# The last group of a fused convolution and MLP kernel: evictions shared by two engines, two closings halved

## The chip, the cores and the metric

The kernel runs on one core of a Trainium2 chip. The metric is the device time of one execution in microseconds. Five engines matter: TensorE (PE; its weight loads are shown as PEld), VectorE (DVE), ScalarE (ACT), GpSimd (POOL, which here computes a little and issues the accumulating transfers), and SyncE (SP, which issues plain transfers). TensorE writes its results to PSUM, eight banks of 512 float32 words in each partition; VectorE and ScalarE carry them from there to SBUF.

## What is computed

A causal convolution over 7 positions with one softmaxed set of taps per head, then a layer norm, an MLP with relu, and a residual sum, all in float32, for 8 sequences of 4224 positions and 192 channels:

```python
def _attn_ref(x, weight):
    ...
    w = np.exp(weight - np.max(weight, axis=-1, keepdims=True))
    w = w / (np.sum(w, axis=-1, keepdims=True) + 1e-09)
    ...
    out = np.einsum('hk,bskhg->bshg', w, x_unf)

def _moe_ref(x, g_ln, w_ch1, w_ch2):
    mu = np.mean(x, axis=-1, keepdims=True)
    var = np.mean((x - mu) ** 2, axis=-1, keepdims=True)
    xn = (x - mu) / np.sqrt(var + 1e-06) * g_ln
    ch = np.maximum(xn @ w_ch1, 0.0) @ w_ch2
    return (x + ch).astype(np.float32)
```

`w_ch1` is 192 x 768 and `w_ch2` is 768 x 192.

## The kernel before

The positions are cut into groups, most of them 16 rows for each of 128 partitions. The groups run one after another through two stages on TensorE: *up* (the product with `w_ch1`, then relu) and *down* (the product with `w_ch2`). While TensorE works on group g, VectorE runs the convolution of group g + 1, ScalarE starts that of g + 2, and POOL and SP move data. The order of every instruction is written out by hand: each engine takes its own in the order of the program, and waits that follow from the data are put in where one engine needs another's result.

From the fourth group on, both stages use a scheme of seven block products instead of eight (of the Strassen kind). In `up_mixed` the hidden matrix is split into four quarters c11, c12, c21, c22, all in one large buffer, `room`. Every product goes into a set of four PSUM banks, X or Y in turn (`take_set`, all eight banks in two sets). The seven products are made twice: in pass *one* for a small part of the hidden width (`n` = 1 block of 128, 1024 words a partition over four banks), in pass *two* for the rest (`n` = `PAIR` = 2 blocks, 2048 words a partition).

Three helpers of `Pass` take a product out of its banks. `evict` (L640) copies it to `room` on ScalarE, with a relu or without. `close` (L644) adds it to a quarter that is there already: with `part` = None VectorE adds straight from PSUM (L648); with a `part` ScalarE copies to that room, and POOL issues a transfer that adds the room to the quarter (`add_by_dma`, L609). `relu` (L655) is ScalarE's, in place. `seen` gives the view of the banks, whole or one block f of it; block f lies in columns 256 f to 256 f + 255 of each of the four banks.

The two rooms of pass two (L693) use the buffers of the tiles "cs" and "tb". "cs" also holds the down results of the previous group until `finish_fast` (called from `ahead`, L986) has added the last parts (L897) and transposed them (L899) into `ots`. This runs between the passes: `next(ahead)` stands at L691.

In the last group (`last`) there is no next group, so VectorE has no convolution to run. c11 (L698) and c22 (L722) of pass two are closed by VectorE whole, each 2048 words from PSUM. In the middle of pass two VectorE also multiplies the previous group's result by the norm's factors (L709), and POOL adds it to the output in HBM in four transfers of 384 KB (`add_to_out`, L925); the transfers that POOL issues, these and `add_by_dma`, share one queue.

After that `down_fast` runs seven products too, over quarters of the hidden matrix. Each goes through `product` (L830), in three chunks c, each with a bank. The first uses c11 and the second `a[:, 1, 0]`, which is relu(c21) less c11 (`lower_sum`, L811). The third, on `a[:, 1, 1]` = relu(c22), accumulates over the banks of the second, so it has to wait until ScalarE has copied the second's result (L841). Then VectorE makes nine sums of quarters (`half_sum`, L802) for the last products. Four rows are kept out of the scheme (`keep`, L749) and computed plainly at the very end (L772), where `add` (L929) and `store` (L936) finish.

Of the kernel before, what the change touches and what calls it, by code (L numbers as in the profile page):

```python
# [10 lines left out]
AF = mybir.ActivationFunctionType  # L11
ALU = mybir.AluOpType
# [4 lines left out]
def kernel(  # L17
# [29 lines left out]
    nc = tc.nc  # L47
# [35 lines left out]
    PAIR = NF // 2 - 1  # L83
# [10 lines left out]
    def rows_of_out(g, j1, j2):  # L94

        b, j0, n = groups[g]
        if b is not None:
            return [(slice(0, P), outr[b, :, (j0 + j1) * D : (j0 + j2) * D])]
        left = out[:, P * R : S].rearrange("b (p r) d -> b p (r d)", p=LP)
        return [  # L100
            (slice(LP * b, LP * b + LP), left[b, :, j1 * D : j2 * D]) for b in range(B)
        ]
# [22 lines left out]
    def take_set():  # L125
        i = (turn[0] + 3) // 4 * 4 % 8
        turn[0] = i + 4
        return all_banks[:, i : i + 4]
# [357 lines left out]
    def store_y(g, queue=nc.sync):  # L486
        n = groups[g][2]
        for ps, rows in rows_of_out(g, 0, n):
            queue.dma_start(out=rows, in_=y[g][ps, 0:n].rearrange("p j d -> p (j d)"))
# [118 lines left out]
    def add_by_dma(dst, src):  # L608
        nc.gpsimd.dma_start(out=dst, in_=src, accum_op=ALU.add)  # L609

    def up_mixed(g, ahead, pending):
# [3 lines left out]
        last = g + 1 == NG  # L615
# [7 lines left out]
        class Pass:  # L623
# [15 lines left out]

            def evict(self, banks, dst, relu=False, f=None):  # L640
                src = self.seen(banks, f)
                nc.scalar.activation(dst, src, AF.Relu) if relu else nc.scalar.copy(dst, src)  # L642

            def close(self, c, banks, part=None, f=None):  # L644


                if part is None:
                    nc.vector.tensor_tensor(c, c, self.seen(banks), op=ALU.add)  # L648
                    return
                self.evict(banks, part, f=f)  # L650
                whole = "p f q w -> p (f q w)"
                add_by_dma(c.rearrange(whole), part.rearrange(whole))
# [4 lines left out]
        def parts(pool, tag):  # L657

            room = pool.tile([P, J * D], F32, tag=tag, name=f"parts_{tag}{g}")
            return room.rearrange("p (f q w) -> p f q w", q=NQ, w=W)  # L660

        def act_scales(j1, j2):
            if not last:
                scale(g - 1, j1, j2)

        def taps_of_next(*args, **kw):
            if not last:
                conv(g + 1, *args, **kw)


        X, Y = take_set(), take_set()
        one, two = Pass(PAIR, FC, X, Y), Pass(0, PAIR, Y, X)
        p = one
# [18 lines left out]
        p = two  # L692
        rooms = parts(cpool, "cs"), parts(bpool, "tb")  # L693
        p.product(Y, a11, p.b11, True, False)
        p.evict(Y, p.c11)
        p.product(X, a12, p.b21)
        if last:
            p.close(p.c11, X)  # L698
        else:
            for f in range(PAIR):  # L700
                p.close(p.c11[:, f : f + 1], X, rooms[0][:, f : f + 1], f)
            if g == 3:
                store_y(g, nc.gpsimd)
        act_scales(0, 1)
        if last:

            for j1 in (0, HJ):
                part, factor = ots[g - 1][:, j1 : j1 + HJ], rstd[g - 1][:, j1 : j1 + HJ]
# [10 lines left out]
        p.product(Y, s1, p.b12, False, False)  # L719
        taps_of_next(2, 5)  # L720
        taps_of_next(5, 6, heads=(0, H // 2))
        p.close(p.c22, Y, None if last else rooms[1][:, 0:PAIR])  # L722
        p.product(X, a22, p.t[2], False)
        for f in range(PAIR):
            p.relu(p.c11[:, f : f + 1])
# [8 lines left out]
        p.product(Y, s4, p.b22, False)  # L734
        p.evict(Y, p.c12, True)
        if last:
            p.relu(p.c22)
        lower_sum(g, range(PAIR))
        if last:

# [65 lines left out]
    def lower_sum(g, fs=range(FC)):  # L806

        a = of_products(g)
        if g in MIXED:
            for f in fs:  # L810
                nc.vector.scalar_tensor_tensor(  # L811
                    out=a[:, 1, 0, f], in0=a[:, 1, 0, f], scalar=0.0, in1=a[:, 0, 0, f],
                    op0=ALU.max, op1=ALU.subtract,
                )
        else:
            half_sum(g, (1, 0), (1, 0), (0, 0), ALU.subtract, fs)
# [174 lines left out]
    for g in range(NG):  # L991
        mixed, last = g in MIXED, g + 1 == NG
        if g + 2 < NG and g not in (1, 2, 3):
            load_x(g + 2)
        if mixed:
            work = up_mixed(g, ahead(g), pending)
            pending = iter(())
        else:
            up(g)
            work = []  # L1000
# [90 lines left out]
```

## Time and profile before

| What | Value |
|---|---|
| Median of 3 runs | 957.46 us (956.49 to 957.8) |
| The profiled execution, in all | 959.62 us |
| Its span, first to last instruction | 957.5 us |
| TensorE matmuls busy | 950.6 us (99%) |
| VectorE busy | 890.7 us (93%) |
| ScalarE busy | 696.6 us (73%) |
| POOL busy | 338.4 us (35%) |
| Up stage of the last group, on TensorE | 896.62 to 924.91 us |
| Down stage of the last group, on TensorE | 924.91 to 953.67 us |
| VectorE in pass two of the last group | first closing at 911.76 us, idle 8.01 us before it |

Times inside the profile are counted from the start of the span. "PE busy" says little, since matmuls are pipelined; the wait ahead of a weight load and the time from one product to the next say more. "L648" is line 648 of the kernel. In a timeline row "[0.29 <-DVE room L648]" means that the engine was idle for 0.29 us and that VectorE's write of `room` on that line ended the wait.

### The profile page before, as it was taken

To read this page: it belongs to the slowest core of one execution; us is meant where nothing else is said; L and a number is where in the kernel's file an instruction comes from. 1 tells how busy PE (TensorE), PEld (TensorE's weight loads), DVE (VectorE), ACT (ScalarE), POOL (GpSimd) and SP (SyncE) were. 2 spreads that over 40 slices of the span, in tenths; PEclk is the share of its full clock that TensorE was granted. 3 is DMA by queue.
4 is the path that set the end of the run, shared out by engine and by line. 5 is a ranking of instruction groups with operands and counts; after the bars stand their busy time and mean duration, and the time that the engine had idled before them with its cause. 6 is when DMAs were issued, how large, how long until landed. Compare 5 with 4: busy or idle time off the path is not lost.

```text
span 957.5 us, 37878 instructions
## 1 busy us (share of the span) xinstructions
PE 950.6 (99%) x16858; PEld 743.1 (78%) x16858; DVE 890.7 (93%) x1489; ACT 696.6 (73%) x1165; POOL 338.4 (35%) x472
## 2 busy tenths in 40 slices
PE   9999999999999999999999999999999999999998
PEld 8998896876869697787968778695867769586787
DVE  7999999999999998999999999999999999999757
ACT  6853678596877959687795968779695877967462
POOL 1058422623145141533227141452316232261310
PEclk9999999999999999999999999999999999999999
DMA  8359589689697988979697896969889696778251
GB/s 204 101 160 212 98 230 280 121 187 229 135 263 138 249 156 181 224 132 277 127 249 151 196 220 127 278 131 252 155 197 205 124 276 132 175 136 138 42 96 68
DMA packets 39544, 168.82 MB, mean 176 GB/s; under 512 B 4437, under 2 KB 8150, under 8 KB 33367
## 3 DMA queue, kind: packets, MB, share of 16 engines
q0 software_dynamic: 32576, 106.25, 59.8%
q1 hardware_dynamic: 6800, 60.16, 17.3%
q8 instruction: 132, 2.16, 0.9%
q14 instruction: 30, 0.25, 0.1%
q10 hardware_dynamic: 6, 0.00, 0.0%
HBM read 38.93 MB, written 50.33 MB: 93 GB/s over the span
## 4 chain that ended last, share of the span: by engine, by line
PE 97%; POOL 1%; DMA 1%; ACT 0%; issue 0%; DVE 0%; ACTq 0%; POOLq 0%
PE ps L533 47%; PE ps L835 44%; PE ps L772 4%; PE ps L367 1%; DMA room<-room 1%; PE ps L326 1%; ACT room L642 0%; POOL room L609 0%; POOL d L460 0%; PE ps L354 0%; POOL r L483 0%; POOL d L479 0%; DVE yt L428 0%; POOL d L478 0%; PE ps L335 0%
## 5 line engine op out<-in xcount | busy, mean ns | idle before, releaser
L417 DVE SCALAR_TENSOR_TENSOR y<-xg,taps,y 128x384 f32<-128x384 f32 (+3 forms) x720 | 364.8, 583 | 1.9 <-DMA y<-room 1.3
L835 PE MATMUL ps<-room,w2sums 128*32 128x256 f32 (+2 forms) x4608 | 247.4, 371 | 0.0
L533 PE MATMUL ps<-yt,w 32*128 32x256 f32 (+2 forms) x4104 | 234.8, 378 | 0.3 <-DVE yt L428 0.3
L642 ACT COPY room<-ps 128x1024 f32<-128x1024 f32 (+1 forms) x135 | 175.0, 1296 | 78.6 <-PE ps L533 77.8
L533 PEld LDWEIGHTS ps<-yt,w 32*128 32x128 f32 x4104 | 204.1, 185 | 25.8 <-issue 8.7
L835 PEld LDWEIGHTS ps<-room,w2sums 128*32 128x32 f32 x4608 | 153.5, 110 | 87.8 <-ACT room L655 5.3
L835 PE MATMUL ps<-room,w 128*32 128x256 f32 (+2 forms) x3456 | 189.8, 371 | 0.1
L802 DVE TENSOR_TENSOR room<-room 128x1024 f32<-128x1024 f32 (+2 forms) x147 | 161.2, 1172 | 22.7 <-PE ps L835 16.1
L835 PEld LDWEIGHTS ps<-room,w 128*32 128x32 f32 x3456 | 113.9, 110 | 67.9 <-DVE room L648 5.0
L533 PE MATMUL ps<-ysums,w1sums 32*128 32x256 f32 x2160 | 125.3, 379 | 0.2 <-issue 0.2
L533 PEld LDWEIGHTS ps<-ysums,w1sums 32*128 32x128 f32 x2160 | 109.1, 185 | 11.2 <-ACT room L642 3.6
L925 POOL DMA_DIRECT2D out_dram<-ot x69 | 58.9, 940 | 159.3 <-ACT ot L914 102.6
L409 POOL DMA_DIRECT2D y<-tb x59 | 52.4, 1384 | 155.0 <-ACT room L841 110.2
L841 ACT COPY cs<-ps 128x256 f32<-128x256 f32 (+2 forms) x192 | 70.2, 367 | 45.6 <-PE ps L835 45.5
L655 ACT ACTIVATE room<-room 128x1024 f32<-128x1024 f32 (+1 forms) x89 | 92.5, 1072 | 0.8 <-DMA room<-parts_cs 0.8
L914 ACT ACTIVATE ot<-ot,r 128x192 f32<-128x192 f32 x224 | 90.9, 464 | 0.0
L380 ACT ACTIVATE y<-xg,taps 128x384 f32<-128x384 f32 (+3 forms) x141 | 73.1, 608 | 0.2 <-DMA xg<-in_x_dram 0.2
L448 DVE BATCH_NORM_STATS2 st<-y 128x6 f32<-128x192 f32 x264 | 70.1, 344 | 0.0
L841 ACT COPY room<-ps 128x256 f32<-128x256 f32 (+2 forms) x96 | 35.5, 369 | 46.5 <-PE ps L835 43.8
L398 ACT ACTIVATE tb<-xg,taps 128x384 f32<-128x384 f32 (+1 forms) x120 | 66.0, 627 | 0.0
L533 PE MATMUL ps<-yt,w1sums 32*128 32x256 f32 x1080 | 65.3, 380 | 0.4 <-ACT room L642 0.4
L533 PE MATMUL ps<-ysums,w 32*128 32x256 f32 x1080 | 64.6, 376 | 0.0
(113 smaller groups left out, 918.0 us busy)
## 6 DMA issues: line engine op xcount, KB each, us to landing
xg<-in_x_dram SPq DMA_DIRECT2D x14, 2112.0 KB, 16.6
room<-room POOLq DMA_DIRECT2D x45, 512.0 KB, 5.1
out_dram<-ot POOLq DMA_DIRECT2D x59, 384.0 KB, 9.6
y<-tb POOLq DMA_DIRECT2D x58, 384.0 KB, 8.5
out_dram<-y SPq DMA_DIRECT2D x13, 1536.0 KB, 9.5
room<-parts_cs POOLq DMA_DIRECT2D x28, 512.0 KB, 6.8
room<-parts_tb POOLq DMA_DIRECT2D x14, 1024.0 KB, 7.6
xg<-in_x_dram POOLq DMA_DIRECT2D x1, 2112.0 KB, 13.6
```

The lines of the kernel that those rows point to most:

```text
L380: nc.scalar.mul(y[g][:, 0:n, cs], xg[g][:, 0:n, cs], taps[:, h, 0:1])
L398: nc.scalar.mul(tb[g][:, 0:n, cs], xg[g][:, 1 : 1 + n, cs], taps[:, h, 1:2])
L417: nc.vector.scalar_tensor_tensor(out=y[g][:, 0:n, cs], in0=t[:, k : k + n, cs], scalar=taps[:, h, k : k + 1], in1=y[g][:, 0:n, cs], op0=AL ...
L448: nc.vector.bn_stats(out=sums[g][:, j, :], in_=y[g][:, j, :])
L533: nc.tensor.matmul(banks[:, q, i * w : i * w + w], right[rows, c, P * i : P * i + P], left[rows, :, c, :], start=(first and c == 0 and i = ...
L642: nc.scalar.activation(dst, src, AF.Relu) if relu else nc.scalar.copy(dst, src)
L655: nc.scalar.activation(c, c, AF.Relu)
L802: nc.vector.tensor_tensor(a[:, *dst, f], a[:, *left, f], a[:, *right, f], op=op)
L835: nc.tensor.matmul(dst[C * q : C * q + C, 0:w], right[:, f, C * c : C * c + C], left[:, f, q], start=(first and f == PAIR), stop=(f == PAI ...
L841: nc.scalar.copy(to[:, c], dst[:, 0:w].rearrange("p (j t) -> p j t", t=t))
L914: nc.scalar.mul(ots[g][:, j, :], ots[g][:, j, :], rstd[g][:, j : j + 1])
L925: nc.gpsimd.dma_start(out=rows[:, d0:d1], in_=src[:, d0:d1], accum_op=ALU.add)
```

## The change

All of it concerns the last group. In pass one each eviction is cut in two by banks: ScalarE takes banks 0 and 1 of the set, VectorE banks 2 and 3, with relu or without; a closing of pass one, which evicts into a room first, is cut the same way. In pass two the closings of c11 and c22 are cut by blocks f: VectorE adds block 0 from PSUM, and ScalarE copies block 1 to a room, from which a transfer on POOL's queue adds it. The relu of c22 is made per block. Because VectorE takes its instructions in order, L897 and L899 of the previous group now come behind its evictions of pass one.

```diff
             def evict(self, banks, dst, relu=False, f=None):
                 src = self.seen(banks, f)
+                if last and self.n == 1:
+                    near, far = [[v[:, :, q : q + 2] for v in (dst, src)] for q in (0, 2)]
+                    if relu:
+                        nc.scalar.activation(*near, AF.Relu)
+                        nc.vector.tensor_scalar_max(*far, 0.0)
+                    else:
+                        nc.scalar.copy(*near)
+                        nc.vector.tensor_copy(*far)
+                    return
                 nc.scalar.activation(dst, src, AF.Relu) if relu else nc.scalar.copy(dst, src)
...
                 if part is None:
-                    nc.vector.tensor_tensor(c, c, self.seen(banks), op=ALU.add)
+                    nc.vector.tensor_tensor(c, c, self.seen(banks, f), op=ALU.add)
                     return
...
         p.product(X, a12, p.b21)
-        if last:
-            p.close(p.c11, X)
-        else:
-            for f in range(PAIR):
-                p.close(p.c11[:, f : f + 1], X, rooms[0][:, f : f + 1], f)
-            if g == 3:
-                store_y(g, nc.gpsimd)
+        for f in range(PAIR):
+            part = None if last and f == 0 else rooms[0][:, f : f + 1]
+            p.close(p.c11[:, f : f + 1], X, part, f)
+        if g == 3:
+            store_y(g, nc.gpsimd)
...
-        p.close(p.c22, Y, None if last else rooms[1][:, 0:PAIR])
+        if last:
+            for f in range(PAIR):
+                p.close(p.c22[:, f : f + 1], Y, rooms[1][:, f : f + 1] if f else None, f)
+        else:
+            p.close(p.c22, Y, rooms[1][:, 0:PAIR])
...
         p.evict(Y, p.c12, True)
         if last:
-            p.relu(p.c22)
+            for f in range(PAIR):
+                p.relu(p.c22[:, f : f + 1])
         lower_sum(g, range(PAIR))
```

## The prediction, made before the changed kernel was run

> **What bounds the kernel now.** I read the busy shares first, then the chain of work that ended last, then the timeline of the last group (896 us to the end), then the landing times of its transfers.
>
> ```profile
> PE 97%; POOL 1%; DMA 1%; ACT 0%; issue 0%; DVE 0%; ACTq 0%; POOLq 0%
> ```
>
> TensorE carries 97% of the chain that sets the end. The last pieces of that chain, in order of time (start, us, engine, tile, line, matmul records):
>
> ```profile
> 859.89 9.28 PE ps L533 x172
> 869.17 27.44 PE ps L835 x504
> 896.62 28.29 PE ps L533 x504
> 924.91 20.76 PE ps L835 x504
> 945.66 8.01 PE ps L772 x48
> ```
>
> Undisturbed up records take 9.28/172 = 54.0 ns each, so 504 cost 27.2 us. The last group's 504 take 28.29: about 1.1 us of waiting lies in the whole up stage, and that is nearly all there is to win. The timeline (start, us, engine, line, operation, tiles, form, idle before and its releaser) shows the places:
>
> ```profile
> 898.03 0.94 DVE L897 TENSOR_TENSOR cs<-cs,room 128x768 f32<-128x768 f32 x1
> 898.19 1.01 ACT L642 COPY room<-ps 128x1024 f32<-128x1024 f32 x1 [1.14 <-PE ps L533]
> 899.01 1.90 DVE L899 STREAM_TRANSPOSE ot<-cs 128x512 f32<-128x512 f32 x3
> 899.25 1.18 PEld L533 LDWEIGHTS ps<-ysums,w1sums 32*128 32x128 f32 x24 [0.24 <-ACT room L642]
> ...
> 911.45 5.53 PE L533 MATMUL ps<-ysums,w1sums 32*128 32x256 f32 x96
> 911.76 2.29 DVE L648 TENSOR_TENSOR room<-room,ps 128x2048 f32<-128x2048 f32 x1 [8.01 <-PE ps L533]
> 913.97 3.42 DVE L709 TENSOR_TENSOR ot<-ot,r 128x1536 f32<-128x1536 f32 x2
> 914.10 2.47 PEld L533 LDWEIGHTS ps<-ysums,w1sums 32*128 32x128 f32 x48 [0.29 <-DVE room L648]
> ...
> 926.75 1.90 ACT L655 ACTIVATE room<-room 128x2048 f32<-128x2048 f32 x1
> ...
> 927.90 6.06 PE L835 MATMUL ps<-room,w2sums 128*32 128x192 f32 x144
> 928.55 0.97 ACT L841 COPY cs<-ps 128x192 f32<-128x192 f32 x4
> ...
> 933.74 7.91 DVE L802 TENSOR_TENSOR room<-room 128x768 f32<-128x768 f32 x9 [6.62 <-ACT kept L749]
> ```
>
> The reader should see four things. A set of four banks is handed back to TensorE some 0.05 us after its eviction ends (898.19 + 1.01 = 899.20, weights at 899.25). VectorE runs the previous group's sums and transposes (L897, L899) during pass one. ScalarE applies the relu to c22 at 926.75 and copies the first down results only behind it. And from 927.90 to the end TensorE has no gap worth naming, while VectorE starts its nine half sums when the third down product has ended and is busy without a break into the last stores. So whatever shifts that third product shifts the end by as much.
>
> **Pass one.** Its seven products are 24 records each, 7 x 24 x 54 ns = 9.07 us. It runs from 896.55 to 906.27 (911.45 less 96 records of the next pass), 9.72 us. So 0.65 us can go if the bank sets come back sooner. Seven ScalarE evictions of 1024 at 1.01 become 14 of 512. ScalarE: 1.01 for 1024 and 1.87 for 2048 give 0.86 per 1024 plus 0.15, so 0.58. VectorE: reading a bank it takes 2.29 for 2048 and 0.35 for 192 (L875), 1.045 ns an element, so 0.68; its bounds are 0.35, the shorter of these reads, and 1.01, the whole eviction of today. With 0.68 each set is back 0.33 us earlier, more than the 0.1 us each product waits. I take the full -0.65; at 1.01 it would be 0.
>
> **The late sums.** VectorE works in order, and its pass-one evictions now stand ahead of L897 and L899, which cost 0.94 + 1.90 + 0.92 + 1.90, 5.7 us with their gaps (898.03 to 903.75). Pass one ends on TensorE at 905.62, its last eviction is ready 0.3 later (906.40 today against 906.1) and ends at 906.6; the sums end at 912.3. Hidden until then by nothing being asked of VectorE: today it idles 8.01 us ahead of 911.76. The cover runs out by 1.2 us, since the c11 closing is ready at 905.62 + 5.18 + 0.3 = 911.1.
>
> **The c11 closing.** VectorE adds one half, 1.22 by the slope above (between 0.35 and 2.29): 912.3 to 913.5. ScalarE copies the other half to the room in "cs", 1.01 (128x1024 row), then one more transfer on POOL's queue. That room is what the late transposes read, so the copy can't begin before 912.3 either. The halves are the two column halves of the same four banks. No row has both engines reading one bank at once: every set goes from one user to the next. The copy starts between 912.3 and 913.5; I take 913.5, nearest to what every handover in the trace looks like, so it ends at 914.5. The third product of pass two then starts at 914.6, today 914.10: +0.5, and the 0.65 is gone. With both halves together it would start at 913.55.
>
> The Trainium skill, "PSUM — Partial Sum Buffer", section "PSUM bank collisions raise a hardware error", speaks against this edit: two engines on the same bank and partitions collide, reads against reads included, and a compiler puts a dependency between them. No row here shows such a pair; by that rule the halves run one after another and the closing gains nothing, and without it TensorE would be 1.05 us earlier here.
>
> **The c22 closing.** Ready at 914.6 + 2 x 2.59 + 0.3 = 920.1; VectorE to 921.3, ScalarE to 922.35, so the last product starts at 922.4 (today 922.03). The c21 closing is unchanged: fourth product over at 922.4, 0.2 more, 2.29 of L648, 0.33 to the weights as today (924.51 to 924.84): down starts at 925.2, today 924.84. The third down product could begin at 925.2 + 3.1 + 2.92 = 931.2, today 927.90 + 2.92 = 930.82. So far +0.4.
>
> **The two transfers.** Each is 512 KB with accumulate, issued by POOL (0.88 each), into the queue that also takes the four 384 KB transfers of the previous group's output (L925). How this queue behaves under a burst (from issue to landing, us), for those four, issued 916.02 to 918.22:
>
> ```profile
> DMA to landing us min/median/max: 4.9/9.0/10.7
> ```
>
> and for the four of y<-tb issued 834.73 to 836.35:
>
> ```profile
> DMA to landing us min/median/max: 4.1/7.4/9.4
> ```
>
> They land one after another: the last is in at 918.22 + 10.7 = 928.9, 12.9 us after the first was issued; for y<-tb at 845.7, 11.0 after. A 512 KB transfer behind another adds 2.6 (parts_cs: issued 857.60 and 858.51, landed after 6.9 and 8.6). Now the c11 half goes in first, at 914.6; POOL issues the four outputs behind it from 915.5 (L709 starts 0.5 earlier); the c22 half is issued at 922.4 behind all of them. It lands at 914.6 + (11.0 to 12.9) + 2 x 2.6 = 930.8 to 932.7. A transfer into SBUF lands sooner than one to HBM (4.1 against 4.9 for the first of each burst), so I take 931.2. If it waited for nobody: 922.4 + 4.5 (the alone row at 910.41) = 926.9. The c11 half lands near 919.5, before its relu at about 922.4: hidden, though it delays the outputs.
>
> **The wait that this adds.** Relu of c22 is now two of 1.06 (128x1024 row) instead of 1.90, +0.1 where nothing waits. The second half needs the transfer; it stands on ScalarE at about 928.2, and behind it, in order, are the three copies of the first down product and the copy of the second's first bank, which the third product accumulates over. Relu 1.06 and four copies 0.97 (the row at 928.55) give landing + 2.0. The third product starts at 933.2 instead of 930.82. This price vanishes if the transfer lands by 929.2 (931.2 less 2.0).
>
> **Sum,** against today, at each place along TensorE: -0.65 at the end of pass one, +0.5 at pass two's third product (the late sums and the halves in series take back 1.15), +0.4 at the start of down and at the earliest start of its third product, and 933.2 - 931.2 = +2.0 there for the transfer: +2.4 us. The profiled execution has a span of 957.5 and 959.62 us in all, 2.1 around the span; the median of the runs shown is 957.46. I add the change to that: **959.9 us**.
>
> **Rivals.** *(a) The same wait, shorter.* The halves run together (third product 913.55 instead of 914.6), the c11 half is issued at 913.4, and the landing comes at 929.5 to 930.5: third down product 931.5 to 932.5, +0.7 to +1.7, so 958.2 to 959.2. For it: the two column halves share no words. Against: no such overlap in the trace.
> *(b) The transfer is in time: not slower.* One mechanism, on POOL's queue: if the c22 half does not stand behind the outputs it lands by 927 and ScalarE never waits. It decides from a landing at 928.0 down, with the halves together (third product at 930.05, less 2.0). Then pass one keeps its -0.65, pass two's handovers give 0.1 more, and the third product stands at 930.05 for 930.82: 956.7. For it: the bulk of the outputs has moved by 927 (DMA busy 0.87 in 925 to 927, 0.11 in 927 to 929). Against: the bursts above land strictly in turn.
> *(c) The burst is slower still,* landing 933 to 934: third product +4.2 to +5.2, 961.7 to 962.7. For it: the first two outputs of the burst land 4.3 us apart (issued 916.02 and 916.56, 4.9 and 8.6 to landing).
> *(d) The closing does nothing by itself:* VectorE half then ScalarE half is 2.2 against 2.29, so TensorE gets the set no sooner. That is in my forecast already; alone, with the transfer in time, it gives +0.4: 957.9.
>
> **How the numbers follow.** Forecast 0.52 (own range 959.0 to 961.5), (a) 0.20, (b) 0.10, (c) 0.10, (d) 0.08. About 0.2%, 1.9 us, is what a measurement can tell from no change; so slower begins at 959.4. Slower: 0.43 of the forecast, all of (c), a little of (a), 0.56. Same: 0.09 + 0.17 + 0.07 + 0.08, 0.40 rounded down. Faster would need more than the 1.2 us that waits offer up to 927.90: 0.04. The range 956.9 to 962.0 leaves out the better part of (b) and the far end of (c).
>
> **What would show it.** ScalarE idle ahead of the second c22 relu, released by a DMA from the tile "tb", ending near 931; TensorE idle ahead of the third down product, released by ScalarE's copy L841; L897 starting near 906.6 instead of 898.03; pass one in about 9.1 us; in the c11 closing the ScalarE copy starting after VectorE's add ends. I am wrong if the c22 half lands by 928, if the copy and the add overlap, or if pass one stays at 9.7 because a VectorE eviction takes 1 us.

## The result, and the profile after

| | before | changed |
|---|---|---|
| Median, 22 runs each | 957.7 us | 959.22 us |
| Ratio, 95% interval | | 1.0018 [1.0011, 1.0025] |
| Span of the profiled execution | 957.5 us | 958.0 us |
| Last group's first up product begins at | 896.55 us | 894.81 us |
| from there to the end of the span | 61.0 us | 63.2 us |

By the ratio the change costs 1.7 us (1.1 to 2.4); the two medians differ by 1.5. The two spans differ by less, because the last group began 1.7 us earlier in the profile of the changed kernel; in the profiles of this study it began anywhere from 893.1 to 896.6 us, and what lies ahead of it no edit here touches. So times below are counted from the first up product of the last group: it ends 2.2 us later.

The end of the chain of waits, in order of time (start, us, what), is no longer TensorE alone:

```profile
920.85 8.37 DMA room<-parts_tb
929.22 0.02 issue
929.24 0.02 ACT room L664
929.27 0.94 issue
930.21 0.97 ACT cs L853 x4
931.18 0.04 issue
931.22 14.83 PE ps L847 x360
946.05 8.01 PE ps L784 x48
```

The transfer of the c22 half takes 8.37 us, the relu of that half follows (the chain books most of it as "issue", time in which ScalarE waits for nothing that the profile shows), then four copies, and only then TensorE's third down product, from which the chain runs on without a break. The timeline shows the same wait from each engine's side, and the steps ahead of it:

```profile
896.54 0.69 DVE L649 COPY room<-ps 128x512 f32<-128x512 f32 x1 [0.18 <-PE ps L533]
...
904.86 0.95 DVE L909 TENSOR_TENSOR cs<-cs,room 128x768 f32<-128x768 f32 x1
...
910.43 1.18 DVE L657 TENSOR_TENSOR room<-room,ps 128x1024 f32<-128x1024 f32 x1
911.53 3.41 DVE L716 TENSOR_TENSOR ot<-ot,r 128x1536 f32<-128x1536 f32 x2
911.64 1.01 ACT L651 COPY parts_cs<-ps 128x1024 f32<-128x1024 f32 x1 [2.97 <-DVE room L657]
912.55 1.87 ACT L651 COPY room<-ps 128x2048 f32<-128x2048 f32 x1
912.71 2.47 PEld L533 LDWEIGHTS ps<-ysums,w1sums 32*128 32x128 f32 x48 [1.19 <-ACT parts_cs L651]
...
929.24 1.06 ACT L664 ACTIVATE room<-room 128x1024 f32<-128x1024 f32 x1 [2.87 <-DMA room<-parts_tb]
930.21 1.40 ACT L853 COPY cs<-ps 128x192 f32<-128x192 f32 x6
931.22 2.76 PEld L847 LDWEIGHTS ps<-room,w2sums 128*32 128x32 f32 x72 [2.00 <-ACT cs L853]
931.22 3.13 PE L847 MATMUL ps<-room,w2sums 128*32 128x192 f32 x72 [1.62 <-ACT cs L853]
...
934.15 7.91 DVE L814 TENSOR_TENSOR room<-room 128x768 f32<-128x768 f32 x9 [8.43 <-ACT kept L761]
```

The reader is to see the previous group's sums begin at 904.86, behind the last of VectorE's evictions; ScalarE's copy in the c11 closing begin at 911.64, when VectorE's add of the other half has ended (910.43 + 1.18 = 911.61); ScalarE idle for 2.87 us until a transfer lands; and TensorE idle until ScalarE's copy. The four output transfers, from issue to landing:

```profile
DMA to landing us min/median/max: 6.8/8.5/11.2
```

### The profile page after: what moved, and what is told of

Its sections match the earlier page's. It is cut to its first block, busy times and chain, and to the rows that moved or that the text cites. A ratio compares the mean times of both kernels' runs of the same rounds, so it can differ in the third digit from the quotient of the medians.

```text
span 958.0 us, 37895 instructions
## 1 busy us (share of the span) xinstructions
PE 947.6 (99%) x16858; PEld 735.5 (77%) x16858; DVE 893.3 (93%) x1496; ACT 695.5 (73%) x1168; POOL 340.0 (35%) x474
## 4 chain that ended last, share of the span: by engine, by line
PE 94%; POOL 2%; DMA 2%; issue 1%; ACT 0%; DVE 0%; POOLq 0%; ACTq 0%
PE ps L533 44%; PE ps L847 44%; PE ps L784 4%; DMA room<-parts_tb 1%; PE ps L367 1%; DMA room<-room 1%; PE ps L326 1%; POOL room L609 1%; POOL out_dram L937 0%; ACT room L651 0%; POOL d L479 0%; POOL d L460 0%; POOL d L478 0%; POOL r L483 0%; PE ps L354 0%
## 5 line engine op out<-in xcount | busy, mean ns | idle before, releaser
L847 PEld LDWEIGHTS ps<-room,w2sums 128*32 128x32 f32 x4608 | 150.7, 110 | 93.1 <-ACT room L664 5.3
L651 ACT COPY room<-ps 128x1024 f32<-128x1024 f32 (+1 forms) x129 | 169.0, 1310 | 73.2 <-PE ps L533 72.1
L847 PEld LDWEIGHTS ps<-room,w 128*32 128x32 f32 x3456 | 111.1, 110 | 70.2 <-DVE room L657 5.0
L664 ACT ACTIVATE room<-room 128x1024 f32<-128x1024 f32 x90 | 92.8, 1063 | 4.3 <-DMA room<-parts_tb 2.9
L609 POOL DMA_DIRECT2D room<-room x45 | 39.4, 876 | 70.9 <-ACT room L651 65.2
```

The source lines that it names most:

```text
L664: nc.scalar.activation(c, c, AF.Relu)
L847: nc.tensor.matmul(dst[C * q : C * q + C, 0:w], right[:, f, C * c : C * c + C], left[:, f, q], start=(first and f == PAIR), stop=(f == PAI ...
```

## The experiments

All edits are to the changed kernel. Times are from the last group's first up product, read from the timeline rows; where rows run together, a product's start is worked out from its neighbour (48 up records 2.59 us, 72 down records 2.92). "Fourth of pass two" is when TensorE gets the set that the c11 closing frees. It is the fourth of the seven products of that pass; the prediction and the expectations call it the third, with the times of the fourth. "Third of down" is the product that needs c22. Each row of the table has one profile, and the intervals of most timed ratios overlap, so the readings rest on the rows of the profiles first.

| Kernel | fourth of pass two | third of down | end | ratio to before, 95% interval |
|---|---|---|---|---|
| before | 17.55 | 34.3 | 61.0 | |
| changed | 17.9 | 36.4 | 63.2 | 1.0018 [1.0011, 1.0025] |
| e1, c22 whole | 17.9 | 34.6 | 61.4 | 1.0010 [1.0001, 1.0019] |
| e2, c11 whole | 17.9 | 36.1 | 62.9 | 1.0035 [1.0023, 1.0047] |
| e3, both whole | 17.9 | 34.6 | 61.4 | 1.0009 [1.0001, 1.0018] |
| e4, outputs later | 17.9 | 34.6 | 61.9 | 1.0014 [1.0005, 1.0023] |
| e5, pass one whole | 17.5 | 36.1 | 62.9 | 1.0013 [1.0003, 1.0023] |
| e6, c11 by banks | 16.9 | 35.8 | 64.2 | 1.0028 [1.0014, 1.0042] |
| e7, c11 on ScalarE | 16.9 | 33.9 | 60.6 | 0.9990 [0.9981, 0.9999] |
| e8, banks, outputs later | 16.9 | 33.4 | 60.4 | 0.9989 [0.9979, 0.9999] |
| e9, c11 by banks, c22 whole | 16.9 | 33.6 | 60.3 | 0.9990 [0.9981, 0.9999] |
| e10, c22 all by transfer | 17.9 | 39.8 | 68.0 | 1.0071 [1.0052, 1.0090] |
| e11, as e2 | 17.9 | 36.3 | 63.0 | one run, 960.99 us |
| e12, as e2 | 17.9 | 37.2 | 64.0 | 1.0031 [1.0020, 1.0042] |

**e1: the c22 transfer taken out.**

```diff
-        if last:
-            for f in range(PAIR):
-                p.close(p.c22[:, f : f + 1], Y, rooms[1][:, f : f + 1] if f else None, f)
-        else:
-            p.close(p.c22, Y, rooms[1][:, 0:PAIR])
+        p.close(p.c22, Y, None if last else rooms[1][:, 0:PAIR])
```

> The changed kernel with c22 closed whole by VectorE again, so without the second transfer. My theory, that the loss is ScalarE's wait for that transfer: no wait ahead of the second c22 relu, the third down product starts 34.5 to 34.7 us after the last group's first up product (before 34.2, changed 36.3), time within 0.5 us of before. Rival, that the late sums and the halves in series cost it: the third down product stays beyond 35.8 and the time 1.5 us or more above before.

The chain of waits of this run ends, in order of time:

```profile
912.42 10.80 PE ps L533 x192
923.22 20.82 PE ps L843 x504
944.04 8.01 PE ps L780 x48
```

TensorE runs the down stage through in 20.82 us, as before (20.76), and the third down product is where the theory had it. The wait is gone with its transfer, and 0.4 us of the loss remains in the profile; e3 below has the same 0.4. The timed ratio, 1.0 us above before, lies above the 0.5 I had expected, with an interval (0.1 to 1.8) that holds it.

**e2, e11, e12: the c11 transfer taken out.**

```diff
-        for f in range(PAIR):
-            part = None if last and f == 0 else rooms[0][:, f : f + 1]
-            p.close(p.c11[:, f : f + 1], X, part, f)
-        if g == 3:
-            store_y(g, nc.gpsimd)
+        if last:
+            p.close(p.c11, X)
+        else:
+            for f in range(PAIR):
+                p.close(p.c11[:, f : f + 1], X, rooms[0][:, f : f + 1], f)
+            if g == 3:
+                store_y(g, nc.gpsimd)
```

> The changed kernel with c11 closed whole by VectorE again, so with the c22 transfer alone. My theory, that the c22 transfer stands behind the four outputs and those start about 1.2 us later now: it lands 33.5 to 35 us after the last group's first up product (changed 34.3), the wait of 2 us stays to within 0.8, time 1 to 2.5 us above before. Rival, that the c11 transfer ahead of the outputs is what makes it late: it lands 2 to 2.6 us sooner and the wait is gone, time within 0.5 us of before.

The wait stays, so the rival falls: it isn't the c11 transfer alone that makes the c22 half late. The outputs start 1.1 us later here, behind the whole add, and the c22 half lands 8.1 us after its issue, 34.1 from the first up product, almost as in the changed kernel (8.4, 34.4). The timing, 3.4 us above before (2.2 to 4.5), was worse than the 1 to 2.5 expected and worse than its profile, so the same kernel was profiled once more and then timed again.

> The kernel with c11 closed whole once more, for a second profile: its timed runs lay 3.3 us above before, though its profile has an end of 62.9 us, only 1.9 above before. If the granted clock falls in some executions and not in others, a second profile has either the same 62.9 with a clock of 1.0 or about 64.5 with a clock of 0.5 for some us behind the wait. If neither, the difference has another cause.

> The kernel with c11 closed whole, timed again: two profiles have an end of 62.9 and 63.0 us after the last group's first up product, 1.9 and 2.0 above before, but its first timing lay 3.3 us above. If that was the chance of few runs, the ratio is now 1.0015 to 1.0025; if some executions lose another 1.5 us to a lower granted clock, it stays at 1.003 or more and its times spread over 4 us again.

The granted clock was 1.0 in all three profiles. What differs in them is the landing: 8.1, 8.2 and 9.1 us after the issue, which moves the third down product from 36.1 to 37.2 and the end from 62.9 to 64.0. The timed runs, whose mean granted clock is recorded, show a second thing: in three of e2's ten executions it was 0.998, as in the profile of e6 below, where the clock was halved for 3.4 us, and these three were its slowest (961.6, 963.06 and 963.12 us). Without them e2's median is still 960.25, 2.9 us above before. In e12 the clock was 0.999 or 1.0 throughout, and its 3.0 us agree with the end of its own profile. So the landing accounts for up to 1.1 us and the clock goes with the slowest runs of e2. What puts the other timed runs some 3 us above before, where two of the three profiles have 1.9 and 2.0, stays open: a landing as late as e12's would do it, but a timed run shows no landing.

**e3: both transfers taken out.** The edits of e1 and e2 together.

> The changed kernel with c11 and c22 both closed whole by VectorE again: pass one halved and the late sums alone. My theory: pass one gains 0.45 us, the late sums give it back at the c11 closing (VectorE free at 15.65 us after the last group's first up product, 2.29 more for the whole add), so pass two's third product starts near 17.9 (before 17.6), the third down product near 34.6 without a wait, end near 61.4 (before 61.0): 0.3 to 0.5 us above before. Rival, that halving pass one is a gain by itself which the closings spoil: third product by 17.2, time 0.3 us or more below before.

The chain of waits of this run, around the c11 closing:

```profile
908.06 0.41 issue
908.47 0.67 DVE ot L909
909.14 2.18 DVE room L657
911.32 0.04 issue
911.36 10.80 PE ps L533 x192
```

As the theory had it: pass one halved saves nothing by itself, since VectorE is held by the late sums (the transposes of L909) when c11 is to be closed (L657), and TensorE waits for the closing. The end is at 61.4; the timing, 0.9 us above before (0.1 to 1.8), holds the 0.3 to 0.5 expected.

**e4: the c22 transfer ahead of the outputs.**

```diff
                 )
-                add_to_out(g - 1, j1, j1 + HJ)
         p.product(Y, s2, p.t[0], False, False)
...
                 p.close(p.c22[:, f : f + 1], Y, rooms[1][:, f : f + 1] if f else None, f)
+            add_to_out(g - 1, 0, J)
         else:
```

> The changed kernel with the four output transfers issued behind the c22 transfer instead of ahead of it. If the place in the queue makes it late: it lands 4.5 to 5.5 us after its issue (changed 8.4), ScalarE doesn't wait, the third down product starts near 34.6 us after the last group's first up product, time within 0.5 us of before. Rival, that a transfer with accumulate is too slow here by itself: landing still 7 us or more after issue, time 1.5 us or more above before.

The same transfer, in the list of transfers of this run (size, us to landing):

```profile
room<-parts_tb POOLq DMA_DIRECT2D x1, 512.0 KB, 5.0
```

and of the changed kernel:

```profile
room<-parts_tb POOLq DMA_DIRECT2D x1, 512.0 KB, 8.4
```

Only the outputs were moved, from ahead of it to behind it, and it lands 3.4 us sooner; nothing waits for it. The DMA engines had as much to do meanwhile: their share was 1.08 and 0.99 from 921 to 923 and from 923 to 925 us here, 1.07 and 1.11 in the changed kernel. So it is the turn in the queue that counts. The timing, 1.3 us above before (0.5 to 2.2), is above the 0.5 expected. Another 0.5 us of the end (61.9, where e1 has 61.4) is lost later, in the fourth down product:

```profile
931.79 2.92 PE L847 MATMUL ps<-room,w 128*32 128x192 f32 x65 [0.43 <-issue]
```

TensorE is idle there for nothing that the profile shows, while the outputs, now later, are under way. e8 has a smaller gap at the same product (0.16). The cause was not tried.

**e5: pass one evicted by ScalarE alone.** The branch for `last and self.n == 1` in `evict` is removed.

> The changed kernel with pass one evicted by ScalarE alone again, so that VectorE makes the previous group's sums early. Theory: pass one takes 9.65 us again instead of 9.09, the c11 closing starts without waiting for the sums, but its halves still run one after the other, so pass two's third product starts near 17.4 us after the first up product (before 17.5, changed 17.8), and the wait for the c22 transfer stays: third down product near 36, time 1.3 to 2.3 us above before. Rival, that the late sums are what costs: time within 0.5 us of before.

The fourth product of pass two is back at 17.5, no earlier than before the change although c11 is closed in halves: 1.2 and 1.0 us in a row are worth no more than 2.29 in one piece. The wait for the c22 half stays, and with it most of the loss in the profile (62.9, where before has 61.0). The timing, 1.2 us above before (0.3 to 2.2), agrees with this without proving it.

**e6: the c11 closing cut by banks.**

```diff
-        for f in range(PAIR):
-            part = None if last and f == 0 else rooms[0][:, f : f + 1]
-            p.close(p.c11[:, f : f + 1], X, part, f)
-        if g == 3:
-            store_y(g, nc.gpsimd)
+        if last:
+            src, far = p.seen(X), rooms[0][:, 0:PAIR, 2:4]
+            near = p.c11[:, :, 0:2]
+            nc.vector.tensor_tensor(near, near, src[:, :, 0:2], op=ALU.add)
+            nc.scalar.copy(far, src[:, :, 2:4])
+            add_by_dma(p.c11[:, :, 2:4], far)
+        else:
+            for f in range(PAIR):
+                p.close(p.c11[:, f : f + 1], X, rooms[0][:, f : f + 1], f)
+            if g == 3:
+                store_y(g, nc.gpsimd)
```

> The changed kernel with the c11 closing cut by banks (VectorE banks 0 and 1 of both blocks, ScalarE banks 2 and 3) instead of by blocks. If the halves run one after the other because they share banks: the ScalarE copy now starts with VectorE's add, and pass two's third product starts near 17.0 us after the first up product instead of 17.9; the wait for the c22 transfer stays, third down product 35.4 to 36.4. Rival, that something else orders the two engines: copy still behind the add, third product at 17.9.

Two neighbouring rows of its timeline:

```profile
912.00 1.18 DVE L709 TENSOR_TENSOR room<-room,ps 128x1024 f32<-128x1024 f32 x1
912.17 1.01 ACT L710 COPY parts_cs<-ps 128x1024 f32<-128x1024 f32 x1 [1.91 <-DVE ot L917]
```

The same amounts of work now overlap; the copy starts when the late transposes have freed its room. In e8 (below), where c22 is cut in the same way, both halves start in the same instant:

```profile
917.31 1.22 DVE L737 TENSOR_TENSOR room<-room,ps 128x1024 f32<-128x1024 f32 x1 [2.28 <-PE ps L533]
917.31 1.01 ACT L738 COPY parts_tb<-ps 128x1024 f32<-128x1024 f32 x1 [0.65 <-PE ps L533]
```

So it was the cut by blocks, with both engines in the same banks, that put the halves of the change in a row. It was a wait in the program: in the changed kernel ScalarE's copy is released by the end of VectorE's add (L657). By blocks the words of the two halves also alternate within the set, by banks they don't; the runs do not separate this from the banks themselves, and whether the chip would have stood both reads at once was not tried. TensorE gets the set 1.0 us sooner. The wait for c22 behind it was longer (landing 8.8 us after issue), and something new followed. Windows of 2 us (busy and count of each engine, then granted clock, DMA share, GB/s):

```profile
930.00:932.00 2.00, 0.18 (x5) 0.00 (x0) 0.00 (x0) 1.75 (x5) 0.00 (x0) 1.00 0.00 0
932.00:934.00 2.00, 1.77 (x32) 1.33 (x36) 0.00 (x0) 0.92 (x5) 0.00 (x0) 0.76 0.00 0
934.00:936.00 2.00, 2.00 (x31) 1.34 (x27) 0.00 (x0) 0.72 (x4) 0.00 (x0) 0.50 0.03 8
936.00:938.00 2.00, 2.00 (x50) 1.57 (x45) 1.16 (x2) 1.15 (x5) 0.00 (x0) 0.89 0.00 0
```

After an idle of 2.05 us TensorE's clock was granted at half, and the third down product took 4.63 us instead of 2.92. Not every execution of e6 had this: the mean granted clock was 0.998 in four of its ten timed runs, this one among them (961.4 to 962.7 us), and 0.999 or 1.0 in the other six (957.0 to 959.9 us).

**e10: a longer wait.** To see whether that clock belongs to the wait, c22 is closed wholly by a transfer:

```diff
-        if last:
-            for f in range(PAIR):
-                p.close(p.c22[:, f : f + 1], Y, rooms[1][:, f : f + 1] if f else None, f)
-        else:
-            p.close(p.c22, Y, rooms[1][:, 0:PAIR])
+        p.close(p.c22, Y, rooms[1][:, 0:PAIR])
```

> The changed kernel with both blocks of c22 copied by ScalarE and added by one transfer of 1024 KB, so that TensorE's wait ahead of the third down product grows by some 2.6 us, to about 4. If a wait costs only its length: end 65.5 to 66 us after the last group's first up product, granted clock 1.0 throughout. If TensorE's granted clock falls after a wait of 2 us or more, as in the run with c11 cut by banks (0.50 for 3.4 us after an idle of 2.05 us): clock 0.5 for some 3 us after the wait, end 67 to 67.5, time 6 us or more above before.

```profile
931.00:933.00 2.00, 0.06 (x4) 0.07 (x8) 0.00 (x0) 2.00 (x8) 0.00 (x0) 0.88 0.00 0
933.00:935.00 2.00, 2.00 (x28) 1.27 (x32) 0.00 (x0) 0.32 (x2) 0.00 (x0) 0.50 0.00 0
935.00:937.00 2.00, 2.00 (x44) 1.36 (x40) 0.00 (x0) 1.01 (x4) 0.00 (x0) 0.76 0.00 0
937.00:939.00 2.00, 2.00 (x60) 1.47 (x52) 1.67 (x2) 1.66 (x6) 0.00 (x0) 1.00 0.03 8
```

The half clock is there again, after 5.1 us idle (I had expected 4), and all four timed runs have a mean clock of 0.998 or less. From the third down product's start to the end it is 26.8 us in the changed kernel and 28.2 here: the clock costs 1.4 us on top of the wait.

**e7, e8, e9: versions without the losses.** e7 closes c11 by ScalarE alone, through the room in "tb", and c22 by VectorE whole; e8 cuts both closings by banks and issues the outputs behind c22's transfer; e9 is e6 with c22 closed whole. In all three the relu of c22 is one instruction again.

> Pass one halved as in the change, c11 closed by ScalarE alone through the room in tb with two transfers, c22 closed whole by VectorE. By my theory nothing then waits: VectorE makes the late sums while ScalarE closes c11, and the transfers of c11 have 8 us until their relu. Pass two's third product near 17.1 us after the first up product, third down product 33.6 to 33.9, end 60.3 to 60.6 against 61.0 before: 0.4 to 0.7 us below before. Rival, that two transfers for c11 land too late for its relus: end 61.0 or more.

> Both closings cut by banks and the four output transfers issued behind the c22 transfer: the change with its two losses removed. Theory: third product near 17.0, down starts near 27.7, the c22 transfer lands 5 us after its issue near 25 and holds ScalarE for 0.5 us at most, third down product 33.6 to 34.0, end 60.3 to 61.0: from 0 to 0.7 us below before. If the wait for a transfer has another cause than the queue, the third down product stays beyond 35.

> Pass one halved, c11 closed by banks (VectorE and ScalarE together), c22 closed whole by VectorE: no transfer on the way to the third down product, outputs where they were. Theory: pass two's third product at 16.9 us after the last group's first up product, down starts near 27.6, third down product near 33.6, end near 60.3 against 61.0 before and 63.2 in the change: 0.6 to 0.8 us below before. Rival, that VectorE with the late sums and a whole c22 closing is too slow: third down product beyond 34.2.

All three end as expected (60.6, 60.4 and 60.3), below both kernels; their timed intervals reach up to 0.9999, so they exclude 1 only just. e9, which has no transfer on the way to down, ends its chain so:

```profile
895.14 27.59 PE ps L533 x504
922.73 20.73 PE ps L848 x504
943.47 8.01 PE ps L785 x48
```

The up stage takes 27.59 us, 28.29 before. That is the gain, 0.7 us, and the timed 0.1% agrees (0.1 to 1.8 us). In e7 the relus of c11 wait for its own transfers (ScalarE idle 1.55 us until a landing), which costs it 0.3.

## Why the prediction was right

The forecast was the wait for the c22 half, at 959.9 us; measured 959.22, or 1.7 us above before by the ratio, for 2.4. The measured ratio, 0.18%, lies just inside the 0.2% that I had called no change, which had a chance of 0.40, beside 0.56 for slower; its interval excludes 1. So the mechanism was right, and the likelier of the two classes did not come.

- **Pass one, -0.65.** From 9.72 us to 9.16 (909.15 less 96 records of 54 ns, less 894.81): -0.56. VectorE's half took 0.69, worked out as 0.68; ScalarE's 0.59 for 0.58.
- **The late sums, ending at 912.3**, 15.75 from the first up product: measured 910.51, 15.7. They delay the c11 closing, as said: the product was over at 909.15, the add began at 910.43, 1.0 us later than the 0.3 that such a start takes (1.2 forecast).
- **The halves in series.** Add 1.18 (1.22 forecast), copy behind it. This was a choice between two ends; the trace of after shows it, and e6 and e8 show what it hangs on. The rule of the Trainium skill, "PSUM — Partial Sum Buffer", section "PSUM bank collisions raise a hardware error", which spoke against this edit, agrees with the order seen, to the point that the cut by banks escapes it.
- **Pass two's fourth product, +0.5; down, +0.4.** Measured +0.35 (17.55 to 17.9) and +0.3 (28.3 to 28.6). The working calls this product the third, and the sixth, "over at 922.4", the fourth; the times are those of the right products.
- **The c22 half, landing at 34.65** from the first up product: 34.4. e4 shows the queue to be the cause, e1 the wait to be the loss. The sum took 14.0 us from the issue of the c11 half to the last landing of the outputs (2.6 for the c11 half, 11.4 for the four) and 2.6 for the c22 half behind them; measured 14.0 (912.96 to 915.78 + 11.2) and 2.2. Inside the 14.0 the terms were mis-sized: without a c11 half the four took 11.8, 11.9 and 12.9 us (e2, e11, e12), which leaves 1.1 to 2.2 for the c11 half. The two errors cancelled, and the landing of one kernel varied by 1.0 us between executions, so to hit it within 0.25 was in part luck. e2 says from the other side that the c11 half isn't the cause: without it the landings are at 34.1, 34.3 and 35.2, though the outputs are issued 1.1 us later there.
- **The third down product, +2.4:** +2.1. It starts 2.0 us after the landing, as worked out.

Of the rivals, (b), the transfer in time, is ruled out by the profile. (c), a landing at 36.45 or later, did not come. (d), the closing without worth and the transfer in time, is what e4 has at the third down product: +0.3 (34.6), for +0.4. (a), the halves together, is ruled out for this edit by the start of the copy. e6 has the closing that (a) supposes, and its landing (33.85) and third down product (35.8) lie within what (a) gives (32.95 to 33.95 and 34.95 to 35.95); the slower clock behind it is in no term of the sum.

## What to carry to other kernels

Splitting an eviction over two engines paid here only where the halves lay in different banks; halves of the same banks ran one after the other. Before an add is turned into a transfer, look at what stands ahead of it in its queue and behind its consumer on that engine: here a landing 3.4 us later put the third down product 1.8 us later (e4 against the change). By the rows, 1.0 us of the way from the landing to that product was four copies behind one relu, three of them results of the first down product, which the third doesn't use; no run put them ahead of the relu. And an engine that is called in to help early has its own later work pushed to where it may be needed: the sums that had been free delayed the next closing by 1.0 us.

## What the runs showed of the hardware

TensorE's granted clock fell to 0.50 for 3.4 us after an idle of 2.05 us (e6) and of 5.1 us (e10), costing 1.6 and 1.4 us; after 1.62 (changed), 1.70 (e5) and even 2.40 us (e12) it stayed at 1.00. So the length of the idle alone doesn't decide. The clock record in the traces shows what else does. In all 14 profiles a stretch of one clock lasts a whole number of steps of 3.41 us, except the last one, which the end of the record cuts off: in e6 270 steps at full clock, 1 at half and 7 at full, in e10 271, 1 and 7, in the changed kernel 279 at full. The clock changes on a fixed grid. Here are windows cut along it, e6 first:

```profile
929.62:933.03 3.41, 1.36 (x35) 0.86 (x29) 0.00 (x0) 2.37 (x7) 0.00 (x0) 1.00 0.00 0
933.03:936.44 3.41, 3.41 (x52) 2.33 (x45) 0.00 (x0) 1.27 (x4) 0.00 (x0) 0.50 0.02 5
```

and e12:

```profile
925.67:929.08 3.41, 2.36 (x60) 1.59 (x52) 0.00 (x0) 0.64 (x1) 0.00 (x0) 1.00 0.25 48
929.08:932.50 3.42, 2.08 (x52) 1.69 (x56) 0.00 (x0) 2.37 (x9) 0.00 (x0) 1.00 0.00 0
932.50:935.91 3.41, 3.41 (x92) 2.73 (x88) 2.56 (x3) 2.92 (x10) 0.00 (x0) 1.00 0.02 5
```

In e6 the whole idle lies in one step, in which TensorE is busy for 1.36 us (the first number behind the length), and the step behind it has half the clock. In e12 the longer idle is shared by two steps, busy for 2.36 and 2.08 us, and the clock stays. Over all steps of the 14 profiles the clock was halved behind each with 1.36 us of work or less (in e8 and e9, where the program ends, behind 0.92 and 1.08), and behind none with 1.68 us (e3, 949.22 to 952.63) or more. So a wait of about 2 us cost the clock or didn't by where it fell in the grid. The Trainium skill, "TensorE: Matmul & The Clock Gate", section "What's actually happening", states a free-running activity window of about 3.4 us, and the grid of 3.41 us agrees with it. The limit of about 3 us idle in its section "Why this matters for your kernels" did not hold in e6.

The same transfer in the same kernel landed 8.1, 8.2 and 9.1 us after its issue in three executions (e2, e11, e12), so a wait behind these outputs varied by 1.0 us from one execution to the next.
